# Attention scores: each head of a pair as its own product with 64 stationary columns

## The chip, the cores and the metric

The program runs on one core of a Trainium2 chip. The metric is the device time of one execution in microseconds (us); the median of a few runs is compared. A profile is one further execution, recorded by the hardware profiler.

## What is computed

Four things follow one another: windowed attention over 4 batches of 8 heads, 576 tokens and 64 elements per head; a dense block with a squared ReLU; a gate that picks one of 8 experts for each token; and the expert's two products, scaled by the gate's weight. Cut to what matters here:

```python
scores = (q @ k.T) / sqrt(64)                 # per batch and head
rel = pos[:, None] - pos[None, :]
scores = where((rel >= 0) & (rel < 64), scores, -1e9)
attn = exp(scores - scores.max(-1)); attn /= attn.sum(-1) + 1e-9
x = (attn @ v)                                # heads side by side: 2304 x 512
h = maximum(x @ w_in, 0); x = (h * h) @ w_out
e = argmax(x @ w_gate); out = softmax_weight * (maximum(x @ w1[e], 0) @ w2[e])
```

## The kernel before

**Tiles.** Because of the window, 64 queries need 128 keys. The attention is cut into 36 groups `g` of 64 queries (9 groups per batch), and in each the 8 heads are taken as 4 pairs `hp`. A pair fills 128 rows: one head's 64 elements stand on rows 0 to 63, the other's on rows 64 to 127. The tile of queries is laid out with zeros, so that it is block diagonal: its first 64 columns hold the first head's queries on the upper rows and zeros below, its last 64 columns the second head's on the lower rows and zeros above. One product with 128 rows, 128 stationary columns (the queries) and 128 moving columns (the keys) then gives the scores of both heads, one head on partitions 0 to 63 of the result and the other on 64 to 127. `att_scores` does that 4 times for a group, at line L362, into one bank of 512 columns.

**Steps of a group.** `att_scores` (L362), `att_max` (the mask, L385, and the maximum, L389), `att_exp` (L405), `att_norm` (L412 to L414, GpSimd), `att_transpose` (L420, four 128x128 transposes), `att_evac` (L425), `att_values` (L435) and `att_out` (L164, L165: the result is split into a high and a low float32r part). `att_values` is 8 products with 64 stationary columns each, two for a pair; the one head's result goes to partitions 0 to 63 and the other's to 64 to 127, so the two use different halves of the array's columns. Scores, transposes and values are plain float32. The trace has two records for each float32 product of the scores and of the values and one for each transpose.

**The dense block.** Tokens go in 9 stages `st` of 256 tokens (4 groups each), with 16 slots `f` per stage. `gemm1` (12 products with 256 moving columns into `h`) and `gemm2` (6 products with 512 moving columns into `y`) use `mm3`, lines L168 to L170: float32r products of high and low parts. `square_low` (L480, VectorE) makes the low part `gl` that `gemm2` needs. In the first 130 us the dense weights arrive by DMA and VectorE, ScalarE and GpSimd rebuild them as float32r (L186 to L230, above all L203, L205, L207, L211 on VectorE).

**The first 8 groups** (`g < NE`) differ: the mask is laid into the bank by a bf16 product (L357) on which the scores are added, and the queries are `qfirst` (`qf`), whose columns stand 16 bytes apart because the pair is the innermost axis. Later groups use `q`, laid out by `lay_q` (L334, L336), with neighbouring columns.

**Order.** `chain` gives each step of a group a slot. Inside that, the Tile scheduler sets the order of instructions of each engine from a model of their times, and it may put other products between the four of a group. After the dense block, experts follow (L748, L788), with an order written out by hand on TensorE.

Of the kernel before, what the change touches and what calls it, by code (L numbers as in the profile page):

```python
# [19 lines left out]
P = 128  # L20
# [29 lines left out]
def kernel(  # L50
# [13 lines left out]
    nc = tc.nc  # L64
    B, _, NB, W, HP = qT.shape
# [53 lines left out]
    for half in range(2):  # L119
        rows = slice(half * W, half * W + W)  # L120
# [30 lines left out]
    def psum(tag, bufs):  # L151
        return pr.tile([P, 512], F32, tag, bufs)
# [140 lines left out]
    NE = 2 * QB  # L293
# [8 lines left out]
    def load_q(g, n=1):  # L302
        b, i = divmod(g, NB)
        if g >= NE:
            qd[g] = br.tile([P, W, HP], F32, "qd", 1)
            nc.sync.dma_start(qd[g], qT[b, :, i])
            return
        qt = qfirst[:, g:g + n]
        for j in range(n):
            qk[g + j] = qfirst[:, g + j]  # L310
        if g > 1:
            for part in (qt[:D, :, W:], qt[D:, :, :W]):
                nc.scalar.copy(part, zero[:part.shape[0]].unsqueeze(2).unsqueeze(3).to_broadcast(part.shape))
        else:
            with tc.issue_after(made.ins):
                nc.vector.memset(qt[:D, :, W:], 0.0)
                nc.vector.memset(qt[D:, :, :W], 0.0)
        for half in range(2):
            rows = slice(half * D, half * D + D)
            nc.sync.dma_start(qt[rows, :, half * W:half * W + W, :], qT[b, rows, i:i + n])  # L320

    def lay_q(g):

        qk[g] = er.tile([P, HP, 2, W], F32, "q", 2)
        if g < NE + 2:
            with tc.issue_after(made.ins):
                nc.gpsimd.memset(qk[g][:D, :, 1, :], 0.0)
                nc.gpsimd.memset(qk[g][D:, :, 0, :], 0.0)
        d = qd.pop(g).rearrange("p s h -> p h s")
        for half in range(2):  # L330
            rows = slice(half * D, half * D + D)

            if g < NE + 5:
                nc.scalar.copy(qk[g][rows, :, half, :], d[rows])  # L334
            else:
                nc.gpsimd.tensor_copy(qk[g][rows, :, half, :], d[rows])  # L336
# [4 lines left out]
    def load_k(g, n=1):  # L341
        b, i = divmod(g, NB)
        nc.sync.dma_start(kfirst[:, g:g + n] if g < NB else kring[:, g % 4:g % 4 + n], kT[b, :, i:i + n])
# [7 lines left out]
    def att_scores(g):  # L351
        qt = qk.pop(g)
        k0 = g - 1 if g % NB else g
        if g < NE:
            ps = ybanks[g % 2]
            m = mask_b[:, 0 if g % NB else 1, :].unsqueeze(1).to_broadcast([P, HP, P])
            nc.tensor.matmul(ps.rearrange("p (h k) -> p h k", h=HP), lhsT=ident_b, rhs=m, start=True, stop=False)  # L357
        else:
            ps = psum("a", 2)
        for hp in range(HP):  # L360
            kt = kfirst[:, k0:k0 + 2] if g < NB else kring[:, k0 % 4:k0 % 4 + 2] if k0 % 4 < 3 else kring[:, 3::-3]
            nc.tensor.matmul(  # L362
                ps[:, hp * P:(hp + 1) * P], lhsT=qt[:, :, hp] if g < NE else qt[:, hp], rhs=kt[:, :, hp, :], start=g >= NE, stop=g >= NE or hp == HP - 1
            )
        if NE <= g < NS * QB - 1:
            lay_q(g + 1)
        if NE <= g < NS * QB - 2:
            load_q(g + 2)
        if NB < g < NS * QB - 3:
            load_k(g + 3)  # L370
        probs[g] = ps
# [510 lines left out]
    slot = {c: i for i, c in enumerate(order)}  # L882
    todo = {}
    ON_PE = (att_scores, att_transpose, att_values, gate_rank, early_pick, early_rows, early_tokens)

    def at(i, f, *args):
# [8 lines left out]
    def chain(i, stages, x, gaps, most=2):  # L895
# [8 lines left out]
        return i  # L904

    ATT = (att_scores, att_max, att_exp, att_norm, att_transpose, att_evac, att_values, att_out)
    at(16, load_gates, 0)

# [248 lines left out]
```

## Time and profile before

| | us |
|---|---|
| median of 3 runs | 841.28 (840.61 to 845.0) |
| the profiled execution | 844.22 |
| span of its trace | 842.5 |
| TensorE busy with products | 789.9 (94%) |
| VectorE busy | 546.4 (65%) |
| ScalarE busy | 400.6 (48%) |
| GpSimd busy | 254.6 (30%) |

The span is the time from the first to the last instruction of the program in the trace; 1.7 us of the execution lie around it. PE is TensorE's products, PEld its weight loads, DVE VectorE, ACT ScalarE, POOL GpSimd, SPq SyncE's queue of DMAs. Busy times of products overlap their neighbours' ends, and the ends are modelled; the starts are the better measure of pace.

### The profile page before, as it was taken

To read this page: it belongs to the slowest core of one execution; us is meant where nothing else is said; L and a number is where in the kernel's file an instruction comes from. 1 tells how busy PE (TensorE), PEld (TensorE's weight loads), DVE (VectorE), ACT (ScalarE), POOL (GpSimd) and SP (SyncE) were. 2 spreads that over 40 slices of the span, in tenths; PEclk is the share of its full clock that TensorE was granted. 3 is DMA by queue.
4 is the path that set the end of the run, shared out by engine and by line. 5 is a ranking of instruction groups with operands and counts; after the bars stand their busy time and mean duration, and the time that the engine had idled before them with its cause. 6 is when DMAs were issued, how large, how long until landed. Compare 5 with 4: busy or idle time off the path is not lost.

```text
span 842.5 us, 15052 instructions
## 1 busy us (share of the span) xinstructions
PE 789.9 (94%) x5212; PEld 685.0 (81%) x5212; DVE 546.4 (65%) x1275; ACT 400.6 (48%) x1059; POOL 254.6 (30%) x257
## 2 busy tenths in 40 slices
PE   6888788999999999999999998989999999999894
PEld 5766667988889888889888897878798888888783
DVE  6999996795773946748558478557778654534110
ACT  6986654343443434344443435436677553433211
POOL 5425431112221122211211006164567642320201
PEclk9999999999999999999999999989999999999998
DMA  9854653110211212111110036366667654420101
GB/s 272 278 148 150 200 154 110 38 39 26 82 32 39 66 36 77 32 45 62 40 51 27 26 100 202 126 213 185 205 205 250 220 154 146 124 91 2 50 2 42
DMA packets 50861, 91.51 MB, mean 109 GB/s; under 512 B 8220, under 2 KB 24604, under 8 KB 50752
## 3 DMA queue, kind: packets, MB, share of 16 engines
q1 hardware_dynamic: 44688, 80.43, 30.3%
q0 software_dynamic: 6064, 9.63, 3.4%
q8 instruction: 69, 1.13, 0.5%
q14 instruction: 40, 0.33, 0.1%
HBM read 84.59 MB, written 13.81 MB: 117 GB/s over the span
## 4 chain that ended last, share of the span: by engine, by line
PE 64%; issue 14%; DVE 11%; DMA 6%; ACT 2%; POOL 2%; SPq 0%; POOLq 0%; DVEq 0%; ACTq 0%
PE h L168 10%; PE h L169 10%; PE h L170 10%; PE y L168 9%; PE y L170 9%; PE y L169 9%; DMA stg<-in_moe_w_out 2%; PE a L362 2%; DVE tmp L207 2%; DVE tmp L211 2%; PE a L435 2%; DVE tmp L203 1%; DMA stg<-in_moe_w 1%; PE a L685 1%; PE a L420 1%
## 5 line engine op out<-in xcount | busy, mean ns | idle before, releaser
L168 PE MATMUL h<-xh,w 128*128 128x256 f32 (+3 forms) x864 | 263.0, 305 | 18.4 <-DVE gl L480 14.2
L169 PE MATMUL h<-xl,w 128*128 128x256 f32 (+3 forms) x864 | 254.9, 295 | 0.4 <-DVE xl L997 0.4
L170 PE MATMUL h<-xh,w 128*128 128x256 f32 (+3 forms) x864 | 254.6, 295 | 0.0
L168 PEld LDWEIGHTS h<-xh,w 128*128 128x128 f32 x864 | 164.2, 190 | 37.9 <-DVE gl L480 19.5
L169 PEld LDWEIGHTS h<-xl,w 128*128 128x128 f32 x864 | 164.5, 190 | 8.1 <-DVE xl L997 0.6
L170 PEld LDWEIGHTS h<-xh,w 128*128 128x128 f32 x864 | 164.4, 190 | 2.8
L464 ACT ACTIVATE r<-h 128x256 f32<-128x256 f32 x144 | 55.2, 384 | 201.7 <-PE h L170 194.0
L168 PE MATMUL y<-w,gh 128*128 128x512 f32 x294 | 119.2, 406 | 4.0 <-ACT gh L471 3.9
L772 DVE SCALAR_TENSOR_TENSOR ggl<-h,ggh 128x512 fp32r<-128x512 f32 (+1 forms) x69 | 46.2, 669 | 114.2 <-ACT ggh L771 114.1
L169 PE MATMUL y<-w,gh 128*128 128x512 f32 x294 | 116.4, 396 | 0.0
L473 DVE SCALAR_TENSOR_TENSOR h<-h,r 128x256 f32<-128x256 f32 x144 | 61.3, 426 | 84.4 <-ACT r L464 84.4
L170 PE MATMUL y<-w,gl 128*128 128x512 f32 x294 | 102.3, 395 | 0.5 <-DVE gl L772 0.5
L771 ACT ACTIVATE ggh<-h 128x512 fp32r<-128x512 f32 (+1 forms) x69 | 40.3, 584 | 124.6 <-PE h L170 96.0
L550 DVE SCALAR_TENSOR_TENSOR tmp<-tmp,stg 128x512 f32<-128x512 f32 x128 | 95.6, 747 | 0.8
L336 POOL COPY q<-qd 64x256 f32<-64x256 f32 x46 | 33.5, 729 | 149.7 <-PE a L362 148.4
L168 PE MATMUL y<-w,ggh 128*128 128x512 f32 x170 | 70.8, 416 | 0.6 <-ACT ggh L771 0.6
L170 PE MATMUL y<-w,ggl 128*128 128x512 f32 x170 | 67.6, 398 | 1.4 <-DVE junk L998 1.1
L168 PEld LDWEIGHTS y<-w,gh 128*128 128x128 f32 x294 | 55.6, 189 | 15.4 <-ACT gh L471 6.0
L169 PE MATMUL y<-w,ggh 128*128 128x512 f32 x170 | 67.1, 395 | 0.0
L480 DVE TENSOR_TENSOR gl<-h,gh 128x256 fp32r<-128x256 f32 x144 | 60.4, 420 | 7.7 <-ACT gh L471 1.0
L278 POOL TENSOR_TENSOR w<-stg,w 128x512 fp32r<-128x512 f32 x27 | 36.4, 1354 | 91.6 <-ACT w L277 88.7
L169 PEld LDWEIGHTS y<-w,gh 128*128 128x128 f32 x294 | 55.6, 189 | 9.5
(165 smaller groups left out, 1276.1 us busy)
## 6 DMA issues: line engine op xcount, KB each, us to landing
stg<-in_moe_w SPq DMA_DIRECT2D x45, 512.0 KB, 4.1
stgx<-in_moe_w SPq DMA_DIRECT2D x18, 512.0 KB, 4.5
stg<-in_moe_w_in SPq DMA_DIRECT2D x16, 512.0 KB, 4.3
stg<-in_moe_w_out SPq DMA_DIRECT2D x16, 512.0 KB, 3.9
v<-in_v SPq DMA_DIRECT2D x28, 256.0 KB, 2.6
x_d<-tmp SPq DMA_DIRECT2D x18, 256.0 KB, 2.0
q<-in_moe_w SPq DMA_DIRECT2D x9, 512.0 KB, 4.7
qd<-in_q SPq DMA_DIRECT2D x28, 128.0 KB, 2.1
```

The lines of the kernel that those rows point to most:

```text
L168: nc.tensor.matmul(o, lhsT=ah, rhs=bh, start=first, stop=False)
L169: nc.tensor.matmul(o, lhsT=ah, rhs=bl, start=False, stop=False)
L170: nc.tensor.matmul(o, lhsT=al, rhs=bh, start=False, stop=last)
L207: nc.vector.scalar_tensor_tensor(out=c, in0=high, scalar=-(1 << 30), in1=c, op0=ALU.bitwise_and, op1=ALU.bitwise_or)
L278: rest.tensor_tensor(l[:, a:a + 512], src, h[:, a:a + 512].bitcast(F32), op=ALU.subtract)
L336: nc.gpsimd.tensor_copy(qk[g][rows, :, half, :], d[rows])
L464: nc.scalar.activation(r, gT[st, f][:, :ST], ACTF.Relu)
L473: nc.vector.scalar_tensor_tensor(out=ps[:, ST:2 * ST], in0=ps[:, :ST], scalar=0.0, in1=r, op0=ALU.max, op1=ALU.mult)
L480: nc.vector.tensor_tensor(gl, ps[:, ST:2 * ST], gh.bitcast(F32), op=ALU.subtract)
L550: nc.vector.scalar_tensor_tensor(out=junk, in0=x2sb[tt], scalar=1.0, in1=w, op0=ALU.mult, op1=ALU.mult, accum_out=l[:, t, e:e + 1])
L771: nc.scalar.activation(h[:, :width], hid[f][:, :width], ACTF.Relu)
L772: nc.vector.scalar_tensor_tensor(out=l[:, :width], in0=hid[f][:, :width], scalar=0.0, in1=h[:, :width].bitcast(F32), op0=ALU.max, op1=ALU. ...
```

## The change

For each pair, the one product with 128 stationary columns becomes two with 64: for `half` 0 the first 64 columns of the query tile, into partitions 0 to 63, for `half` 1 the last 64, into partitions 64 to 127. All 128 rows still take part, the zeros too, and the moving operand is the same 128 key columns both times. Nothing else in the text changes; 36 groups have 8 products instead of 4.

```diff
         for hp in range(HP):
             kt = kfirst[:, k0:k0 + 2] if g < NB else kring[:, k0 % 4:k0 % 4 + 2] if k0 % 4 < 3 else kring[:, 3::-3]
-            nc.tensor.matmul(
-                ps[:, hp * P:(hp + 1) * P], lhsT=qt[:, :, hp] if g < NE else qt[:, hp], rhs=kt[:, :, hp, :], start=g >= NE, stop=g >= NE or hp == HP - 1
-            )
+            cols = slice(hp * P, hp * P + P)
+
+            for half in range(2):
+                rows = slice(half * W, half * W + W)
+                nc.tensor.matmul(
+                    ps[rows, cols], lhsT=qt[:, rows, hp] if g < NE else qt[:, hp, half, :], rhs=kt[:, :, hp, :],
+                    start=g >= NE, stop=g >= NE or hp == HP - 1,
+                )
```

The lines below it move by five: the scores are L366 afterwards, the transposes L425, the values L440.

The scheduler answers with another order. From the fifth stage on (18 groups), TensorE's order keeps its shape. There, before (`s` are the normalised scores, `a` the banks of the attention, `h` and `y` the dense block's):

```order
L170 MATMUL y_132<-w_701,gl_83 128x512
L420 MATMUL a_209<-ident,s_1147 128x128 x4
L362 MATMUL a_210<-k,q 128x128 x4
L168 MATMUL h_459<-xh,w_700 128x256
...
L170 MATMUL y_132<-w_701,gl_84 128x512
L435 MATMUL a_209<-s_1147,v_439 64x64 x8
L168 MATMUL h_460<-xh,w_700 128x256
```

And after:

```order
L170 MATMUL y_132<-w_733,gl_83 128x512
L425 MATMUL a_217<-ident,s_1183 128x128 x4
L366 MATMUL a_218<-k,q 64x128 x8
L168 MATMUL h_491<-xh,w_732 128x256
...
L170 MATMUL y_132<-w_733,gl_84 128x512
L440 MATMUL a_217<-s_1183,v_471 64x64 x8
L168 MATMUL h_492<-xh,w_732 128x256
```

The eight narrow score products stand between transposes and dense products, which use all 128 columns; the values stand elsewhere, as before.

In the third and fourth stage (the four groups before those 18), the scheduler breaks the scores into more pieces. On TensorE, the first of these groups before:

```order
L169 MATMUL y_132<-w_703,gh_82 128x512
L362 MATMUL a_209<-k,q 128x128 x3
L168 MATMUL h_459<-xh,w_700 128x256
...
L170 MATMUL y_134<-w_701,gl_83 128x512
L362 MATMUL a_209<-k,q 128x128
L168 MATMUL y_133<-w_701,gh_81 128x512
```

And after:

```order
L169 MATMUL y_132<-w_735,gh_82 128x512
L366 MATMUL a_217<-k,q 64x128 x3
L168 MATMUL h_491<-xh,w_732 128x256
...
L170 MATMUL y_134<-w_733,gl_83 128x512
L366 MATMUL a_217<-k,q 64x128 x4
L168 MATMUL y_133<-w_733,gh_81 128x512
...
L169 MATMUL y_134<-w_735,gh_81 128x512
L366 MATMUL a_217<-k,q 64x128
L168 MATMUL h_491<-xh,w_732 128x256
```

Two pieces became three, one of them a single product without its other half.

Call a visit one unbroken run of products with 64 stationary columns on TensorE, whichever step they belong to. The order of before has 35 visits (all of them values), that of after 77. In the four groups and the 18 they are 24 before and 52 after: 5 and 15 in the stretch of the four, 19 and 37 in that of the 18. In all that lies ahead of these they are 11 and 25.

## Rows read from the trace of the kernel before

**Rows 1.** The page's first part: busy us, share of the span, instructions.

```profile
PE 789.9 (94%) x5212; PEld 685.0 (81%) x5212; DVE 546.4 (65%) x1275; ACT 400.6 (48%) x1059; POOL 254.6 (30%) x257
```

**Rows 2.** Stretches: length, PE, PEld, DVE, ACT, POOL busy (count), granted clock, DMA share, GB/s.

```profile
105.00:126.00 21.00, 17.25 (x116) 13.77 (x114) 21.00 (x39) 11.18 (x22) 7.97 (x6) 1.00 0.49 149
147.00:168.00 21.00, 21.00 (x140) 19.15 (x139) 14.57 (x41) 7.72 (x24) 2.62 (x3) 1.00 0.11 38
462.00:504.00 42.00, 42.00 (x296) 37.76 (x295) 24.02 (x69) 15.65 (x43) 1.47 (x2) 1.00 0.18 56
```

**Rows 3.** All waits of TensorE's products from 126 to 500 us: total, times, longest.

```profile
PE y L168 <- ACT gh L471: 1.5, 1, 1.5
PE h L168 <- DVE gl L480: 1.0, 1, 1.0
```

**Rows 4.** Groups by shape from 126 to 490 us: count | busy us, mean ns | idle before.

```profile
L362 PE MATMUL a<-k,q 128*128 128x128 f32 x176 | 24.1, 275 | 0.0
L435 PE MATMUL a<-s,v 128*64 128x64 f32 x368 | 16.0, 228 | 0.0
```

**Rows 5.** Timeline of PE around one group's scores: start us, us, what, count.

```profile
463.45 0.60 PE L420 MATMUL a<-ident,s 128*128 128x128 f32 x4
463.89 1.06 PE L362 MATMUL a<-k,q 128*128 128x128 f32 x8
...
464.90 0.28 PE L169 MATMUL h<-xl,w 128*128 128x256 f32 x1
465.02 0.28 PE L170 MATMUL h<-xh,w 128*128 128x256 f32 x1
```

**Rows 6.** The same timeline around that stage's next values.

```profile
467.12 0.40 PE L169 MATMUL y<-w,gh 128*128 128x512 f32 x1
467.35 0.39 PE L170 MATMUL y<-w,gl 128*128 128x512 f32 x1
467.67 0.69 PE L435 MATMUL a<-s,v 128*64 128x64 f32 x16
...
468.51 0.28 PE L169 MATMUL h<-xl,w 128*128 128x256 f32 x1
```

**Rows 7.** Records of the two lines: ns min/median/max, first and last start.

```profile
L362 PE MATMUL a<-k,q x216: 270/275/422, 46.0 to 464.7; 128*128 128x128 f32 x108
...
L435 PE MATMUL a<-s,v x448: 222/222/271, 58.9 to 481.3; 128*64 128x64 f32 x150
```

**Rows 8.** The same values in stretches of 0.06 us, L435 alone; columns as Rows 2.

```profile
467.70:467.76 0.06, 0.06 (x2) 0.06 (x4) 1.00 0.68 239
467.76:467.82 0.06, 0.06 (x4) 0.06 (x6) 1.00 0.53 205
467.82:467.88 0.06, 0.06 (x6) 0.06 (x6) 1.00 0.53 205
```

**Rows 9.** Timeline of PE around values that are broken into two pieces.

```profile
175.46 0.34 PE L435 MATMUL a<-s,v 128*64 128x64 f32 x4
175.72 0.50 PE L168 MATMUL y<-w,gh 128*128 128x512 f32 x1
176.06 0.39 PE L169 MATMUL y<-w,gh 128*128 128x512 f32 x1
```

**Rows 10.** Timeline of PE: float32 products of the last gate, 8 moving columns.

```profile
538.64 1.85 PE L530 MATMUL y<-wg,tmp 128*128 128x8 f32 x16
```

**Rows 11.** Timeline of PEld at the beginning: weight loads of the first two groups' scores.

```profile
5.31 3.81 PEld L362 LDWEIGHTS y<-kf,qf 128*128 128x128 f32 x16 [1.33 <-issue]
```

**Rows 12.** The chain that ended last, in order of time: start us, us, what.

```profile
12.50 1.84 PE y L362 x8
...
492.00 0.70 DVE tmp L550 x2
...
493.67 3.46 DMA stg<-in_moe_w
```

**Rows 13.** The longest wait of TensorE's products from 0 to 126 us.

```profile
PE h L168 <- DVE gl L480: 11.6, 11, 1.8
```

## The prediction

> **What bounds the kernel now.** I read the page's busy times first: TensorE's products fill 94% of the span, all others are far behind [rows 1]. That is an average, so the table of stretches comes next [rows 2]. Between 105 and 126 us VectorE is busy for 21.00 of 21.00 us and TensorE for 17.25: that part belongs to VectorE, which rebuilds the dense weights. From 147 to 504 us TensorE is busy for every microsecond, VectorE for little more than half. The waits say it again: from 126 to 500 us TensorE's products waited 1.5 and 1.0 us, once each, and for nothing else [rows 3]. So in that stretch whatever is added to TensorE's row of work goes into the time one for one. The grouped rows give the count there: 176 records of L362 are 22 groups with 8 records each, 368 of L435 are 23 groups with 16 [rows 4].
>
> **What the scores cost now.** From the first start of a score product to the dense product L169 behind it (463.89 to 464.90) 1.01 us pass [rows 5]. The records follow one another by (1.06 - 0.275)/7 = 0.112 us, with the median record of 0.275 [rows 5, 7]; eight make 0.90. A dense product with 256 columns takes 0.12 (464.90 to 465.02). 0.90 + 0.12 = 1.02: going from dense products to 128-column float32 scores and back costs nothing.
>
> **What a visit costs.** The values are the row nearest to the new scores: float32, 128 rows, 64 stationary columns, a half of the array's columns for each head. First, do the halves run side by side? In stretches of 0.06 us, the count of running L435 records rises by two each time: 2, 4, 6 [rows 8]. And 12 more records lengthen a block from 0.34 to 0.69 us [rows 6, 9]: 0.35/6 = 0.058 us for two records. So they come in twos. Second, the edges. From the L170 ahead (467.35) to the L169 behind (468.51) 1.16 us pass [rows 6]. Undisturbed it would be 0.23 for the L170 (467.12 to 467.35), 8 x 0.058 = 0.47 for the values and 0.12 for the L168: 0.82. The visit costs **0.34 us** beside its work. It is the edge that costs, not the length: a block broken in two pays again. From 175.46 to 176.06 a piece of four records took 0.60, of which 2 x 0.058 and 0.23 are work, 0.25 edge [rows 9]; the whole block has 0.84 - 0.47 - 0.12 = 0.25 behind its start too [rows 6], and the remaining 0.09 ahead of it.
>
> The Trainium skill, "TensorEngine Tiling (Array Packing)", section Key Properties, says that a change of the tiling mode drains the engine, and that tiles run independently. It speaks against this change, for it makes 42 more such changes and back. The trace agrees with both halves of it, 0.34 us a visit and records in twos; without the rule the sum below would be 0.45 us.
>
> **The change part by part.** *The products themselves.* Half as many columns stand still, but the keys that stream past are as many, so each record streams as long as before, and two of them run at once. The values stream 64 columns and their median record is 0.222 us, the scores' 128 columns give 0.275 [rows 7]: 53 ns for 64 columns more, 0.83 ns a column. A pair of new records should then take 0.058 + 0.053 = 0.111 us, and eight pairs 0.89 against 0.90: **nothing gained, nothing lost**. The bounds: 0.058 if streaming is not what sets the pace, 2 x 0.112 = 0.224 if the halves take turns. I take 0.111, because it follows the row of the same shape but for the moving columns.
>
> *Edges in the 18 regular groups.* The order leaves the scores alone between transposes and dense products, so each group has two visits for one: 18 x 0.34 = 6.1 us. Entering from a transpose is not in the trace; leaving (0.25 of 0.34) is. If entering were free it would be 4.5, and if it cost twice as much, 7.7.
>
> *Edges in the four irregular groups.* 15 visits for 5: 10 x 0.34 = 3.4 us. In two of these groups an odd piece leaves a product without its other half, so that two records run alone, 2 x 0.112 = 0.22 each time: 0.45.
>
> *Ahead of 126 us.* There are 25 visits for 11, 14 x 0.34 = 4.8 us more of TensorE. Against that, the first 8 groups load weights whose columns stand 16 bytes apart, and there the loads set the pace, 3.81/16 = 0.24 us a record [rows 11]; with halves loaded side by side it may be 0.12 for each of the old records, 8 x 8 x 0.12 = 7.7 us less. Both are put down at **nothing**: VectorE is full there, TensorE waited 11.6 us for its `gl` up to 126 us [rows 13], and only one block of scores, 1.84 us long, stands on the chain [rows 12]. If the cover were gone, it would be between -3 and +5 us. The order of VectorE's work up to its last L211 has one instruction more than before, so its end there should not move.
>
> *Waits.* Each second half in the first groups waits for the DMA of its own rows of `qf`; both had to be there before. `att_max` and `lay_q` wait for the last of the scores, 0.1 us or so later in a slot of several us; VectorE and GpSimd have 24.02 and 1.47 of 42.00 us to do [rows 2]. Nothing there.
>
> *Behind the attention.* After 490 us the chain goes through the gate's dots (L550) and then a DMA of expert weights [rows 12]. The dots need the dense block's result, and the DMA the buffers that the dots free, so both come later by what TensorE is late.
>
> **The sum**: 6.1 + 3.4 + 0.45 = 10.0 us (1.2%). Against the profiled execution 844.2 + 10.0 = 854.2; the median of the runs is 2.9 lower, and there the forecast is 841.3 + 10.0 = **851.3 us**. With the bounds of entering and of the beginning it reaches from 846 to 857.
>
> **Rivals.**
> *Loads set the pace.* The gate's float32 products with 8 moving columns follow one another by 1.85/16 = 0.116 us or less [rows 10], and the scores with 128 by 0.112. So the load of 128 columns, not streaming, might be what sets 0.112; then 64-column loads, side by side, give the values' 0.058 a pair: 0.47 instead of 0.90, 22 x 0.43 = 9.5 us back. The edges are still paid: +0.5, 841.8 us, no change. Against it: the lengths of the records, which grow by 53 ns for 64 columns, though their ends are modelled. Chance 0.07.
> The Trainium skill, "TensorE: Matmul & The Clock Gate", section "LDWEIGHTS (loading the stationary operand)", gives the columns divided by 1.2 as nanoseconds, by which this is estimated at 107 for 128 columns and 53 for 64, and the sum would be this rival's. The page "FP8 and Floating Point Precision", section "TensorE Precision Notes", has true float32 go through the array four times, and by that the sum is the forecast's. The pace of 0.112 agrees with both.
> *Loads, and they hide the edges too* (**faster**). If most of a visit's 0.34 is the exposed first load, and the loads of a free half can be taken ahead, scores have the pace of 0.058 and a small edge p: -9.5 + 28 p. It decides at p = 0.19, below which the gain passes 4.2 us; at p = 0.1 it is -6.7, 834.6 us. Against it: in both pieces of the values the edge was the full one. Chance 0.04.
> *The halves take turns.* If two records with the same keys cannot stream at once, eight pairs take 1.79 for 0.90: 22 x 0.89 = 19.6 more, 871 us. Against it: the values do run in twos [rows 8]. Chance 0.05.
> *The delay is absorbed.* If the DMA on the chain at 493 us [rows 12] is held by something other than the dots, say by loads queued ahead of it on its queue, TensorE's delay would vanish up to its 3.46 us and the queue's wait behind it: about 8 of 10 us, 843 us. Against it: its buffers hold the gate's weights until L550. Chance 0.07.
> That the change doesn't do what it says is excluded by the order: 8 products of 64 columns stand there.
>
> **Chances.** The forecast has 0.77. 0.5% is 4.2 us, about what a measurement of this kernel can tell from no change: faster is below 837.1, slower above 845.5. Faster 0.04; within it 0.07 + 0.07 and 0.02 for the forecast's lower end, 0.16; slower 0.75 + 0.05 = 0.80. The range of 846 to 857 alone holds some 0.73, so it is stretched to 841.5, which takes in the two cases of no change.
>
> **What would show it.** The new score line with 16 records for a group, starting in twos, a pair each 0.11 us: the pace is right; 0.06 would be the loads' rival, singles 0.11 apart the turns'. From the last transpose's start to the L169 behind the scores, about 1.47 us instead of 1.12. The same waits of TensorE from 126 to 500 us, and the last values about 10 us later than 481. It is wrong if the scheduler's order at the beginning makes VectorE wait, or if entering from a transpose costs other than from a dense product.

## The result

The changed kernel takes **848.23 us** (median of 9 runs, 846.56 to 850.97); the kernel before, run beside it, 842.38 (840.61 to 845.0). The ratio is 1.0074, with a 95% interval of 1.0062 to 1.0087: **slower by 6.2 us**, between 5.2 and 7.3. The forecast was slower by 10.0, so the sign and the range hold and the size is 3.8 too large. The profiled execution took 850.97 us, of which 849.2 are its span; that of before took 844.22 and 842.5.

The page's first part and two of its stretches show the bound unchanged (columns as in [rows 1] and [rows 2]):

```profile
PE 798.3 (94%) x5500; PEld 680.7 (80%) x5500; DVE 545.7 (64%) x1275; ACT 401.2 (47%) x1059; POOL 256.5 (30%) x257
```

```profile
105.00:126.00 21.00, 17.98 (x122) 14.54 (x121) 20.71 (x42) 12.84 (x32) 8.25 (x7) 1.00 0.52 165
...
462.00:504.00 42.00, 42.00 (x304) 37.35 (x303) 21.79 (x64) 14.86 (x43) 4.08 (x4) 1.00 0.13 44
```

There are 288 records more than in [rows 1], 36 groups x 8. VectorE is all but full from 105 to 126 us and TensorE has no gap towards the attention's end, as in [rows 2]. The only wait of TensorE's products from 126 to 506 us is of a kind that [rows 3] has too, and the total is about the same (2.1 us for 1.5 + 1.0):

```profile
PE h L168 <- DVE gl L485: 2.1, 2, 1.4
```

One group's scores in the stretch that TensorE bounds, on PE's timeline (start us, us, what, count), and that stage's next values further down:

```profile
469.20 0.39 PE L170 MATMUL y<-w,gl 128*128 128x512 f32 x1
469.44 0.60 PE L425 MATMUL a<-ident,s 128*128 128x128 f32 x4
469.96 1.09 PE L366 MATMUL a<-k,q 128*64 128x128 f32 x16
470.99 0.39 PE L168 MATMUL h<-xh,w 128*128 128x256 f32 x1
471.21 0.28 PE L169 MATMUL h<-xl,w 128*128 128x256 f32 x1
...
474.00 0.69 PE L440 MATMUL a<-s,v 128*64 128x64 f32 x16
474.62 0.39 PE L168 MATMUL h<-xh,w 128*128 128x256 f32 x1
```

Against [rows 5]: from the first score to the second dense product behind it 1.25 us (469.96 to 471.21) instead of 1.01 (463.89 to 464.90), and from the first transpose to the first score 0.52 (469.44 to 469.96) instead of 0.44 (463.45 to 463.89): 0.32 in all. What happens inside the block is seen in short stretches, L366 alone (length, PE and PEld busy with the count of records, clock, DMA):

```profile
470.05:470.11 0.06, 0.06 (x2) 0.06 (x4) 1.00 0.00 0
470.11:470.16 0.05, 0.05 (x4) 0.05 (x4) 1.00 0.00 0
...
470.22:470.27 0.05, 0.05 (x6) 0.05 (x4) 1.00 0.00 0
```

The records come in twos, 2, 4, 6, as the values did in [rows 8]. The records of the new line (ns min/median/max, first and last start) are as long as the full-width ones were in [rows 7], 273 against 275 ns:

```profile
L366 PE MATMUL a<-k,q x432: 272/273/324, 55.7 to 470.8; 128*64 128x128 f32 x144
...
L440 PE MATMUL a<-s,v x448: 219/222/271, 68.4 to 487.7; 128*64 128x64 f32 x150
```

The last start of the values, 487.7, answers to 481.3 in [rows 7]: 6.4 us of delay stand there already, and in this pair of traces, whose spans differ by 6.7, hardly anything is added or absorbed behind it.

**Milestones.** To see where the time went, I cut each trace at four places: the start of the last L211 (VectorE's rebuilding of the dense weights ends), and the starts of the first, the eighth and the ninth copy of the dense block's result (L500 before, L505 after, L503 in kernels with a part of the change; one copy per stage). The rows of the two lines, before and after:

```profile
L211 DVE SCALAR_TENSOR_TENSOR tmp<-stg,tmp x32: 672/678/1787, 11.4 to 136.9; 128x512 int32<-128x512 int32 x32
...
L500 ACT COPY tmp<-y x9: 568/580/589, 155.0 to 536.1; 128x512 f32<-128x512 f32 x9
```

```profile
L211 DVE SCALAR_TENSOR_TENSOR tmp<-stg,tmp x32: 656/680/1528, 11.2 to 134.9; 128x512 int32<-128x512 int32 x32
...
L505 ACT COPY tmp<-y x9: 579/580/588, 151.9 to 542.5; 128x512 f32<-128x512 f32 x9
```

All kernels of the study, in us, from one profiled execution each ("narrow" lists the groups whose scores are 64-column products; merge, merge32 and apart are explained with their experiments):

| kernel | narrow | last L211 | to 1st copy | 1st to 8th | 8th to 9th | behind | span |
|---|---|---|---|---|---|---|---|
| before | none | 136.9 | 18.1 | 334.3 | 46.9 | 306.3 | 842.5 |
| late | 18 to 35 | 136.5 | 18.1 | 339.9 | 45.9 | 305.0 | 845.4 |
| irregular | 14 to 17 | 134.8 | 18.2 | 338.0 | 46.1 | 306.6 | 843.7 |
| from14 | 14 to 35 | 134.6 | 18.3 | 343.7 | 45.8 | 306.1 | 848.5 |
| from14, again | 14 to 35 | 135.5 | 18.3 | 343.7 | 45.8 | 308.8 | 852.0 |
| first8 | 0 to 7 | 136.1 | 19.9 | 334.2 | 46.2 | 304.2 | 840.6 |
| first14 | 0 to 13 | 136.2 | 16.9 | 334.2 | 46.0 | 310.1 | 843.4 |
| first14, again | 0 to 13 | 133.2 | 16.9 | 334.2 | 45.8 | 308.6 | 838.6 |
| first18 | 0 to 17 | 133.3 | 17.0 | 338.0 | 48.5 | 307.5 | 844.2 |
| after | all | 134.9 | 17.0 | 343.7 | 46.9 | 306.7 | 849.2 |
| after, again | all | 135.1 | 17.0 | 343.7 | 45.8 | 306.8 | 848.3 |
| merge | all | 133.3 | 17.0 | 337.7 | 53.5 | 304.8 | 846.4 |
| merge32 | all | 136.4 | 17.0 | 342.4 | 45.5 | 305.3 | 846.5 |
| apart | all | 135.4 | 17.0 | 352.4 | 44.8 | 306.0 | 855.5 |

Two columns repeat to 0.1 us for the same order of instructions, "to 1st copy" and "1st to 8th". The others scatter by some us between executions, so a difference of one pair of profiles there tells nothing by itself. In the two that repeat, the granted TensorE clock is 1.00 in every trace. Elsewhere it falls for some microseconds to 0.50, the lower of its two levels (1.2 and 2.4 GHz): its mean is 0.91 to 0.99 ahead of the last L211 and 0.96 to 0.98 behind the ninth copy, so part of the scatter can come from there. From the eighth to the ninth copy it fell in two traces alone, first18 and merge, which are also the two with the longest times there (48.5 and 53.5). From the first to the eighth copy, where neither kernel leaves TensorE a gap, the change costs 343.7 - 334.3 = **9.4 us**, for 27 of the 28 added visits (one of the irregular groups' lies ahead of the first copy). The timed loss is 3 us smaller than that; the experiments ask about both.

### The profile page after: what moved, and what is told of

Same layout as the page of the kernel before. It is cut to its first block, busy times and chain, and to the rows that moved or that the text cites. A ratio compares the mean times of both kernels' runs of the same rounds, so it can differ in the third digit from the quotient of the medians.

```text
span 849.2 us, 15644 instructions
## 1 busy us (share of the span) xinstructions
PE 798.3 (94%) x5500; PEld 680.7 (80%) x5500; DVE 545.7 (64%) x1275; ACT 401.2 (47%) x1059; POOL 256.5 (30%) x257
## 4 chain that ended last, share of the span: by engine, by line
PE 66%; issue 13%; DVE 13%; DMA 3%; ACT 2%; POOL 1%; SPq 0%; POOLq 0%; DVEq 0%; ACTq 0%
PE h L168 11%; PE h L170 10%; PE h L169 10%; PE y L168 10%; PE y L170 9%; PE y L169 9%; PE a L366 3%; DVE tmp L211 2%; DVE tmp L207 2%; PE a L440 2%; DVE tmp L203 1%; PE a L425 1%; DVE w L278 1%; PE a L690 1%; DVE gl L485 1%
## 5 line engine op out<-in xcount | busy, mean ns | idle before, releaser
L777 DVE SCALAR_TENSOR_TENSOR ggl<-h,ggh 128x512 fp32r<-128x512 f32 (+1 forms) x69 | 46.2, 670 | 114.5 <-ACT ggh L776 114.4
```

The costliest lines, as they stand in the source:

```text
L777: nc.vector.scalar_tensor_tensor(out=l[:, :width], in0=hid[f][:, :width], scalar=0.0, in1=h[:, :width].bitcast(F32), op0=ALU.max, op1=ALU. ...
```

## The experiments

The expectations name theories by letters, which they explain where they first use them. In the discussion I call them the *edge theory* (what was recorded: each visit pays about 0.34 us where TensorE is the bound, nothing elsewhere), the *beginning's gain* (groups 0 to 13 give some 3 us back) and *nothing at the beginning* (they give nothing, and what one pair of profiles shows there is scatter). Ratios are against the kernel before, run on the same chip, with 95% intervals. Microseconds are the ratio less one, times 842.

**One part of the change alone.** The six kernels differ in one condition: which groups take the narrow products.

```diff
-            for half in range(2):
-                rows = slice(half * W, half * W + W)
-                nc.tensor.matmul(
-                    ps[rows, cols], lhsT=qt[:, rows, hp] if g < NE else qt[:, hp, half, :], rhs=kt[:, :, hp, :],
-                    start=g >= NE, stop=g >= NE or hp == HP - 1,
-                )
+            for half in range(2) if g >= 18 else [None]:
+                rows = slice(0, P) if half is None else slice(half * W, half * W + W)
+                w = qt[:, rows, hp] if g < NE else qt[:, hp] if half is None else qt[:, hp, half, :]
+                nc.tensor.matmul(ps[rows, cols], lhsT=w, rhs=kt[:, :, hp, :], start=g >= NE, stop=g >= NE or hp == HP - 1)
```

*The 18 regular groups* (`g >= 18`, as shown):

> Only the 18 regular groups (from group 18 on) have narrow scores; the 18 groups ahead keep one product for each pair. TensorE's order up to group 17 is that of the kernel before. Theory A (each added visit costs its two edges, in the changed kernel's trace 1.246 us instead of 1.014 behind the first score plus 0.202 instead of 0.109 ahead of it, 0.325 us; the products themselves cost nothing): 18 x 0.325 = 5.9 us slower than before, ratio 1.007, and the scores of group 17 start where they did. Rival B (the whole change's 5.9 us is made by these 18 visits and the irregular four, but part of it is given back at the end of the attention by the DMA on the chain): about 3 us slower, with the last values 5.9 us later and the span only 3 longer.

Measured 847.37 us, 1.0068 [1.0044, 1.0092], +5.7 us. The stretch from the first to the eighth copy is 339.9 - 334.3 = 5.6 longer, 18 x 0.31. The edge theory holds for these groups, and rival B's 3 us lies outside the interval (3.7 to 7.7).

*The first fourteen* (`g < 14`):

> Only groups 0 to 13 have narrow scores, those that lie ahead of 126 us; the four irregular and the 18 regular groups keep one product for each pair. TensorE's order is that of the changed kernel up to group 13 and that of before from there. Theory C (the beginning of the changed kernel is really shorter, by some 3 us at 149 us of the trace): 3 to 4 us faster than before, ratio 0.996. Rival D (that was chance in one execution): no difference, ratio 1.000. Rival E (edges count ahead of 126 us too, 14 of them at 0.325): 4.6 us slower.

Measured 843.37 us, 1.0012 [0.9994, 1.0029]: no change that can be told. A gain of 3 us, as the first pair of profiles had suggested, isn't there.

*The first eight* (`g < 8`), where the queries' columns stand 16 bytes apart:

> Only groups 0 to 7 have narrow scores, those whose query columns stand 16 bytes apart. Theory C1 (the gain at the beginning comes from their weight loads, 64 columns at a time): the same 3 us faster as with groups 0 to 13, and TensorE's time for these scores is shorter than before's. Rival C2 (it comes from the order that the scheduler chose around groups 8 to 13, VectorE's above all): less than 1 us, or any other value, and the time of VectorE's last L211 follows it.

Measured 842.64 us, 1.0006 [0.9989, 1.0023]: again nothing.

*The four irregular groups* (`14 <= g < 18`):

> Only groups 14 to 17 have narrow scores, those that the scheduler breaks into pieces; everything ahead and behind is as before, TensorE's order up to them too. Theory A (edges, 10 more visits at 0.33, and two products without their other half at 0.22): 3.7 us slower than before, ratio 1.0045, all of it between the first and the third stage's end in the trace. Rival G (pieces between dense products cost less than whole visits): under 2 us.

Measured 846.56 us, 1.0051 [1.0031, 1.0071], +4.3. Rival G's 2 us lies outside the interval (2.6 to 6.0). From the first to the eighth copy the trace has 338.0 - 334.3 = 3.7 of it: four groups cost two thirds of what the other 18 cost there. On PE's timeline of the changed kernel the pieces into which the scheduler breaks such a group can be seen:

```profile
149.31 0.65 PE L366 MATMUL a<-k,q 128*64 128x128 f32 x6
149.89 0.39 PE L168 MATMUL h<-xh,w 128*128 128x256 f32 x1
150.12 0.28 PE L169 MATMUL h<-xl,w 128*128 128x256 f32 x1
...
154.77 0.66 PE L366 MATMUL a<-k,q 128*64 128x128 f32 x8
155.35 0.50 PE L168 MATMUL y<-w,gh 128*128 128x512 f32 x1
```

Three products take 0.58 us until the dense product behind them starts (149.31 to 149.89), 0.19 each, where a product of a whole group takes (470.99 - 469.96)/8 = 0.13: the edge is shared by fewer, and the third has no other half to run beside. It is the number of pieces that counts: these four groups add nine visits to that stretch.

*Both together* (`g >= 14`):

> Groups 14 to 35 have narrow scores, the 14 ahead of them keep one product for each pair, so the beginning is that of before. Theory A: the sum of both stretches, 5.9 + 3.7 = 9.6 us slower than before, ratio 1.0114, and so 3 us slower than the changed kernel: the forecast's 10 us was right for this part, and the changed kernel's first 14 groups give 3 to 4 back. Rival H (the first 14 groups give nothing, and the stretches together cost less than their sum): 6 us, as the changed kernel.

Measured 851.55 us, 1.0123 [1.0098, 1.0147], +10.4. That is what the prediction had summed up for all of the change, 10.0, and it is some 4 us **more** than the whole change costs. The two parts add up: 5.7 + 4.3 = 10.0.

*All but the regular ones* (`g < 18`):

> Groups 0 to 17 have narrow scores, the 18 regular ones do not; TensorE's order is that of the changed kernel up to group 17. Theory C (a beginning that is 3 us shorter, 3.7 us of edges in groups 14 to 17): 0 to 1 us slower than before. Rival D (nothing is gained at the beginning): 3.7 to 4.8 us slower.

Measured 843.71 us, 1.0022 [1.001, 1.0034], +1.9: less than the four irregular groups alone (+4.3), though its trace has the same 338.0 between the copies. It lies between both expectations. Its interval (0.8 to 2.9 us) just touches that of the four groups alone (2.6 to 6.0), so the run hints at a gain and doesn't show it: the narrow products of the first groups seem to give something back when later ones are narrow, and gave nothing when they were alone.

**The whole, the beginning and the rest once more,** all beside the same runs of the kernel before:

> The changed kernel once more, on one chip with its two parts (groups 0 to 13, and groups 14 to 35). Theory A with a beginning that gives back what the order of the first 14 groups makes (1.2 us from VectorE's last L211 to the end of the first dense stage in all traces of that order): 8.3 us slower than before, ratio 1.0099. Rival I (it gives back the whole difference of 4 us that stands between the first two measurements, 6.2 of the whole and 10.3 of groups 14 to 35): 6.2 us again, and that of groups 14 to 35 stays 4 higher.

> Groups 0 to 13 alone, once more, on one chip with the whole. Theory A: 1.2 us faster than before, ratio 0.9986, near what can be told from none. Rival I: 4 us faster. Rival D: nothing or slightly slower, as at first (1.0012).

> Groups 14 to 35 alone, once more, on one chip with the whole. Theory A: 9.6 us slower than before, ratio 1.0114. If it comes out at the whole's own time, the first 14 groups give nothing.

Measured: the whole 848.66 us, 1.0073 [1.0054, 1.0091]; groups 0 to 13 alone 842.86, 1.0003 [0.9986, 1.002]; groups 14 to 35 alone 851.78, 1.0115 [1.01, 1.0129]. All three repeat. The intervals of the whole and of groups 14 to 35 lie apart, by 0.0042 in the middle, so a gain of 3.5 to 4 us from narrow products in groups 0 to 13 is measured twice; on its own, in the kernel that has nothing else, it measures as none (+0.3 and +1.0).

What the traces show of it is the column "to 1st copy". Five traces whose first 14 groups are as before have 18.1 to 18.3 us from the last L211 to the first copy, eight with them narrow have 16.9 or 17.0 (with the first eight alone narrow it is 19.9, an order of its own). The scheduler orders the beginning otherwise there, and TensorE waits less for `gl` up to 147 us (total us, times, longest). Before, then the changed kernel, then groups 0 to 13 alone and groups 14 to 35 alone:

```profile
PE h L168 <- DVE gl L480: 12.6, 12, 1.8
```

```profile
PE h L168 <- DVE gl L485: 7.0, 9, 1.4
```

```profile
PE h L168 <- DVE gl L483: 6.8, 9, 1.3
```

```profile
PE h L168 <- DVE gl L483: 12.6, 12, 1.7
```

With the first groups narrow more of the dense work is done while VectorE still rebuilds: from the last L211 to the first copy 33 records of `y` are left instead of 39. That accounts for 1.2 us. (Other waits grew, above all those for the first groups' exponentials; all waits of TensorE up to 147 us fall only from 28.0 to 26.1 us.) The rest, 2 to 3 us, I can't place. The last L211 itself starts at 134.6 to 136.9 us with the order of before and at 133.2 to 136.4 with the other, on the mean of the traces 1 us earlier, but these overlap. The granted clock doesn't separate the kernels: its mean over the runs is 0.985 for the whole and for groups 14 to 35 alone.

That groups 0 to 13 alone gain nothing has a part that can be seen. In the three traces with these groups narrow and the regular ones wide (first14 twice, first18), TensorE is idle between its products for 12.3 to 13.4 us behind the ninth copy, in the eleven others for 9.4 to 10.9. What is more stands in the experts, some 93 to 110 us behind that copy, and the profile names nothing that ends these waits ("issue"). The waits there with groups 0 to 13 alone (its second trace, from 618 to 642 us), then before (624 to 650):

```profile
PE h L168 <- issue: 1.2, 2, 0.9
PE y L795 <- issue: 1.0, 1, 1.0
```

```profile
PE y L170 <- DVE junk L998: 0.6, 1, 0.6
PE h L168 <- issue: 0.2, 1, 0.2
```

So these kernels lose 2 to 3 us there; why the experts wait in them, no run shows.

**The edge taken away.** If each visit pays, scores that stand directly behind a group's values, which are 64 columns wide too, should pay no edge of their own. One slot later, the regular groups' scores follow the values of the group before:

```diff
-        chain(i, ATT, g, (0, 1, 1, 1, 1, 1, 0, 1))
+        chain(i + (g >= 18), ATT, g, (0, 1, 0, 1, 1, 1, 0, 1) if g >= 18 else (0, 1, 1, 1, 1, 1, 0, 1))
```

> The changed kernel, with the scores of the 18 regular groups one slot later, so that each stands right behind the values of the group before it: one visit for the two, 59 visits in all instead of 77. The maximum and the exponentials take one slot instead of two, so nothing behind the scores comes later. Theory A (the edges are the cost): 18 x 0.325 = 5.9 us less than the changed kernel, which is 842.4 us, the time of before. Rival F (the cost is that of the narrow products wherever they stand): 848 us, as the changed kernel.

Measured 850.7 us, 1.01 [1.0081, 1.012], slower than the changed kernel, and yet the edges went. The 337.7 us from the first to the eighth copy can't be set against 343.7 as they are, for the two stretches don't hold the same work: 40 of TensorE's records, one block of values and 24 of the dense block, now stand behind the eighth copy. From the first to the ninth copy both have the same 2931 records. These two stretches of the changed kernel, and then of this one (length, PE busy with the count, clock, DMA):

```profile
151.90:542.50 390.60, 388.11 (x2931) 1.00 0.18 58
151.90:495.60 343.70, 343.70 (x2654) 1.00 0.15 44
```

```profile
150.30:541.60 391.30, 384.43 (x2931) 1.00 0.18 58
150.30:488.00 337.70, 334.93 (x2614) 1.00 0.14 45
```

TensorE is busy for 388.1 - 384.4 = 3.7 us less. In this trace the granted clock also stood at 0.50 for 3.4 of these microseconds, shortly behind the longest wait, of 2.9 us:

```profile
524.70:528.10 3.40, 3.40 (x12) 0.50 0.83 313
```

If the work there takes half as long at 1.00, that is 1.7 us, and 18 visits fewer save an estimated 5.4, 0.30 each. PE's timeline of this kernel shows the two kinds of narrow products side by side:

```profile
476.67 0.69 PE L440 MATMUL a<-s,v 128*64 128x64 f32 x16
477.18 1.05 PE L366 MATMUL a<-k,q 128*64 128x128 f32 x16
478.16 0.39 PE L170 MATMUL h<-xh,w 128*128 128x256 f32 x1
478.38 0.40 PE L170 MATMUL y<-w,gl 128*128 128x512 f32 x1
```

477.18 - 476.67 = 0.51 for the values and 0.98 for the scores: 1.49 for both, where they take 0.62 (474.00 to 474.62) and 1.03 apart, besides what is saved ahead of and behind them. What was saved is lost again: from the first to the ninth copy TensorE is idle for 391.3 - 384.4 = 6.9 us instead of 390.6 - 388.1 = 2.5, and the clock's 1.7 come on top. The last groups come a slot later at the end of the attention, and there TensorE waits longest, in the list of waits from 480 to 560 us:

```profile
PE h L168 <- DVE gl L485: 3.5, 2, 2.9
```

So this run confirms the edge by TensorE's busy time and not by its own time. The same with the last stage left as it was (`18 <= g < 32`):

> The scores stand behind the values of the group before in groups 18 to 31 only; the last stage's four groups keep their slots of the changed kernel, so that nothing moves at the attention's end. 64 visits instead of 77. Theory A (edges are the cost, and what the merged kernel lost came from the last stage's later scores): 13 x 0.325 = 4.2 us less than the changed kernel, some 844 us. Rival F (merging gives nothing in total): 848 us or more.

Measured 846.52 us, 1.0052 [1.0034, 1.007], +4.4: 1.8 us better than the changed kernel, where 4.2 had been expected, and the intervals overlap. The same two stretches:

```profile
153.40:541.30 387.90, 384.80 (x2931) 1.00 0.19 58
153.40:495.80 342.40, 340.44 (x2653) 1.00 0.15 44
```

TensorE is busy for 388.1 - 384.8 = 3.3 us less, 0.25 for each of 13 visits fewer. From the first to the eighth copy only 1.3 us of that come out (342.4 for 343.7), since TensorE is now idle there for 2.0 us and wasn't in the changed kernel. The eighth to ninth copy is short again (45.5) and its clock is 1.00, so the long wait and the low clock of the kernel ahead came with the last stage's slot, as far as one trace of each tells. Neither beats the kernel before.

**The halves one after the other.** Do the halves overlap because they alternate, or whatever their order? In the regular groups, all four products of the first half, then all four of the second:

```diff
+        turns = [(hp, half) for hp in range(HP) for half in range(2)]
+        if g >= 18:
+            turns.sort(key=lambda t: t[1])
+        for hp, half in turns:
```

> The changed kernel, but in the 18 regular groups all four products of the one half stand first, then all four of the other. Theory J (two records run at once only if neighbours in the order use different halves): the block of a group takes 16 x 0.109 = 1.74 us instead of 0.87, 18 x 0.87 = 15.7 us more than the changed kernel, 864 us. Rival K (each half of the columns works off its own row of instructions, however they are mixed): the same time as the changed kernel, 848 us.

Measured 857.75 us, 1.0193 [1.0175, 1.021], 9.5 us above the changed kernel's median: neither expectation. The stretch between the copies has 352.4 - 343.7 = 8.7 of it, 0.48 us per group. PE's timeline of a group, and the block of scores cut in three (L366 alone, PE and PEld busy with counts):

```profile
235.30 0.60 PE L425 MATMUL a<-ident,s 128*128 128x128 f32 x4
235.83 1.58 PE L366 MATMUL a<-k,q 128*64 128x128 f32 x16
237.34 0.39 PE L168 MATMUL h<-xh,w 128*128 128x256 f32 x1
```

```profile
235.83:236.32 0.49, 0.49 (x4) 0.49 (x5) 1.00 0.00 0
236.32:236.70 0.38, 0.38 (x9) 0.38 (x8) 1.00 0.00 0
236.70:237.14 0.44, 0.44 (x9) 0.44 (x5) 1.00 0.00 0
```

In the first 0.49 us four records run, all of the first half. At 236.32 the second half's first record starts, the ninth in the program, together with the first half's fifth; from there both halves run, and at the end the second half is alone again. From the first start to the last one there are 1.31 us instead of 0.82. Four steps alone, four together and four alone are twelve steps where the alternating block has eight: 4 x 0.109 = 0.44 more, of the 0.48 measured. All 18 groups show the same steps. The halves overlap here for four steps of the eight that they could; and three records of the first half start later than the second half's first, so the two halves don't keep the program's order between them.

## Why the prediction was right, and where it was off

**What bounds the kernel: right.** TensorE is without a gap from 147 us to the end of the attention, with a wait of the same kind as before, and what was added there went into the time one for one (+9.4 in the stretch; +10.4 and +9.7 when timed alone).

**The products themselves at nothing: right.** The records start in twos, 0.109 us a pair (0.111 was forecast), so eight pairs replace eight records at 0.112. This settles the rivals of the pace: if the loads set it, pairs would start every 0.058 us, and if the halves took turns, single records every 0.11. TensorE's loads are busy for 680.7 us instead of 685.0 with 288 more of them, and the pace stayed. What sets the pace of a 128-column product here is thus not the load's width; the streaming of the keys, as the lengths in [rows 7] had suggested, fits it.

**The edge: right.** In the undisturbed group, first score to second dense product is 0.24 us longer and the entry behind the transposes 0.08: 0.32 a visit, for 0.34 forecast from the values. The entry was the part that [rows 5] didn't show; it costs what it cost the values. 18 x 0.34 = 6.1 measured 5.6 to 5.7, the irregular groups' 3.4 + 0.45 measured 3.7 to 4.3. The two kernels with merged visits have the same narrow products and fewer visits, and saved 0.30 (with an estimate for the clock) and 0.25 us of TensorE's busy time for each visit less, as they must if the edge and not the width is the cost; the size is a little under 0.32. The Trainium skill, "TensorEngine Tiling (Array Packing)", section Key Properties, has a change of tiling mode drain the engine and has tiles run independently. The trace agrees with the first, at about 0.33 us there and back, and with the second only for records that stand close together: half by half, the block took 1.31 us instead of 0.82.

**Behind the attention: right, as far as can be told.** The last values come 6.4 us later and the run is 6.2 us longer; in this pair nothing was absorbed. The forecast had them 10 us later, for the reason that follows.

**The step that was mis-sized: "Ahead of 126 us", put at nothing.** It was the one term taken from an argument (VectorE is full there, so TensorE's work is covered) rather than from rows. Alone it held: groups 0 to 13, with 14 visits more, measured +0.3 and +1.0, which can't be told from none. But beside the narrow later groups the term is a gain of 3.5 to 4 us, just outside its own bound of -3: 10.4 and 9.7 with groups 14 to 35 alone against 6.2 with all. About 1.2 us of it is seen: with another order of TensorE's work the waits for `gl` fall from 12.6 to 7.0 us, and less dense work is left when VectorE is done. The prediction had named the scheduler's order at the beginning as a danger and not as a gain, and had looked only at the order of VectorE's own work. The other 2 to 3 us are not explained. That groups 0 to 13 alone measure no gain goes with 2 to 3 us more of waits in the experts, whose cause is open.

The loads side by side, which the prediction had priced at 0.12 us for each record of before in the first eight groups, can be seen. One group's scores there from the first start to the last (length, PE and PEld busy with counts, clock, DMA), before, then two groups of the changed kernel:

```profile
27.05:28.64 1.59, 1.59 (x7) 1.59 (x8) 1.00 1.08 365
```

```profile
14.50:16.07 1.57, 1.57 (x16) 1.57 (x16) 0.50 1.10 233
26.93:27.87 0.94, 0.94 (x15) 0.94 (x16) 1.00 1.03 375
```

At the full clock a pair of narrow records starts every 0.120 us where single records started every 0.233 before, so the price was right, 0.65 us for a group. But only the last three of the eight groups got it in this trace; the three ahead of them ran at a clock of 0.50, the first of these behind a wait of 4.6 us for exponentials, and gained next to nothing. That is some 2 us of TensorE's time for the 7.7 priced. Whether it has a part in the gain is not shown: the first eight alone gave nothing, but neither did the first fourteen.

## What to carry to other kernels

Two products in one half of the array's columns each took together the time of the one full-width product that they replace, and each unbroken run of them among full-width products pays an edge, here a third of a microsecond; count runs, not products, and put narrow products next to other narrow ones where that makes no engine wait (both merged kernels lost part of the saving to waits). Alternate the halves in program order: one after the other they lost half of their overlap here. A term at nothing because "another engine is the bound" still needs a look at what is left to do when that engine is done, for a scheduler answers a small change with another order.

## What the runs showed of the hardware that was not expected

The overlap of the halves depends on how near they stand: with eight records of one half ahead of the other's first, the second half started after four, ahead of the first half's last three, and the block took 1.31 us for 0.82. A gap of 0.16 us stands between the first pair and the second at the start of a visit (469.96 to some 470.12), 0.05 more than the pace. The weight loads of the visit start with it and not ahead of it (469.96 too), which fits the gap; no run tests it:

```profile
469.96 0.31 PEld L366 LDWEIGHTS a<-k,q 128*64 128x64 f32 x6 [0.17 <-issue]
```

Weights whose columns stand 16 bytes apart held the full-width products at 0.233 us a record; as two halves side by side they went at 0.120 a pair. And a full dense stretch at a granted clock of 1.00 repeats to 0.1 us between executions of a kernel whose total times differ by 3 us and more: 343.7 in four traces with groups 14 to 35 narrow, 334.2 or 334.3 in four with them wide. So a cut of the trace at milestones told more than the medians did, as long as both cuts hold the same records, which the first merged kernel's did not.
